# Moving the query weights to the head of the load stream, and the query ahead of the first key transposes

## Chip, cores and metric

The kernel runs on one core of one Trainium2 chip. The metric is device microseconds of one execution. Before the change the median is 190.97 us (5 runs, 190.83 to 191.34). Of the 95 executions on record, 91 lie within 0.3% of the median of their set; the widest set on record, 11 runs of before, spans 190.66 to 191.81. Every run of this study is on record as fast, so fast runs are compared with fast runs. The experiments ran on two chips, on which before has medians of 190.82 to 190.87 us.

## The reference

One decode step of a gated mix of attention and a small feed-forward network, for 8 rows `x` of 448 numbers:

```python
g = sigmoid((x * gate_w).sum(-1, keepdims=True))
# attention: 16 query heads, 8 key/value heads of 256, the last 1024 positions of the cache
q = (x @ wq)                      # wq is 448 x 4096, 3.67 MB
p = softmax(q . k * 256**-0.5)    # for each batch row and head
a = (p . v) @ wo                  # wo is 4096 x 448
# feed-forward: 448 -> 1792 -> 448
b = gelu(layernorm(x) @ w1 + b1) @ w2 + b2
out = g * a + (1 - g) * b         # 8 x 1 x 448, bf16
```

The window of keys and values is 8 x 8 x 1024 x 256 in bf16, 33.5 MB each. There is little arithmetic for so many bytes.

## The kernel before

All large loads go through one ring of nine slots of 16 KB per partition, issued by the sync engine (SP) in the order of a plan. A slot is loaded again when the entry nine places earlier has been used up (`done`).

```python
def pump():
    while len(slots) < min(len(plan), consumed[0] + RING):     # RING = 9
        t = ring.tile([P, SLOT], BF16, tag="slot", name="slot")
        plan[len(slots)](t)
        slots.append(t)
...
add_kv("k", A_k_cache, 0, parts=2)                     # first keys, 2 transfers of 1 MB
add(("wq", 0), rows_loader([wq_m[:, 0 : 2 * HD]]))     # query weights, 3 transfers, 3.67 MB
add(("wq", 1), rows_loader([wq_m[:, 2 * HD : 3 * HD], wq_t]))
add(("w1",), rows_loader([w1_m, w1_t]))
add(("w2",), rows_loader([w2_v]))
for u in range(1, NQ):                                 # NQ = 16 units of 4 key/value heads
    add_kv("k", A_k_cache, u)                          # 2.1 MB
    if u >= LAG:                                       # LAG = 2
        add_kv("v", A_v_cache, u - LAG)                # 2.1 MB
...                                                    # the last values, then wo in 6 pieces
```

Each unit's keys are turned by VectorE in two halves (`turn_keys`), multiplied by TensorE (`scores`), and used for softmax and values two units later. The query goes through TensorE, ScalarE and VectorE in turn:

```python
def turn_keys(u, hf):
    ...
    nc.vector.transpose(kt[...], kn[:, hf * CH * Dh : (hf + 1) * CH * Dh].bitcast(WORD))
    if hf == NH - 1:
        done()

def query():
    for r in range(NR + 1): ...   # 32 matmuls with wq, into Sq
    done(2)
    nc.scalar.activation(qs[:], Sq[:], ACT.Copy, scale=qscale)
    ...                           # 8 TensorE transposes, 4 VectorE copies (qd), 8 matmuls (qp)
    ...                           # 8 copies into the query tile qw, ScalarE and VectorE in turn

norm_and_gate()
for hf in range(NH):
    turn_keys(0, hf)
query()
hs = mlp_hidden()
for hf in range(NH):
    scores(0, hf)
mlp_out(hs)
for u in range(1, NQ): ...        # the steady state
...                               # the last units, then the output projection with wo
```

## Time and profile before

| | before |
|---|---|
| time, median | 190.97 us |
| span of the profiled run | 189.3 us |
| bytes read from HBM | 77.68 MB |
| load stream by the packet records, first to last byte | 182.8 us, 425 GB/s |
| TensorE / VectorE busy | 71% / 68% |
| last unit's keys landed, first transpose starts | 162.1 us |

The page of before, its slice rows and its chain (the work that ended last, followed back step by step to what released it). Each slice is 4.7 us; a digit is the busy share in tenths. PE is TensorE, PEld its weight loads, DVE VectorE, ACT ScalarE and POOL GpSimd.

```profile
span 189.3 us, 2502 instructions
PE 134.2 (71%) x1013; PEld 69.8 (37%) x1022; DVE 128.1 (68%) x186; ACT 43.1 (23%) x91; POOL 5.0 (3%) x7
...
DMA  5999999999999999999999999999999999999980
GB/s 188 422 424 434 428 435 431 422 422 440 429 433 429 426 436 426 429 436 433 429 426 433 428 436 422 433 433 426 436 426 433 436 426 426 436 433 426 410 356 14
...
DMA 84%; PE 8%; DVE 3%; ACT 1%; SPq 1%; issue 1%; ACTq 0%
```

No compute engine is above 71%, while the DMA row is full from the second slice to the last but two and the rate under it hardly moves. Over the whole stream the rate is 425 GB/s, and the slices but the first and the last three read 422 to 440. (Single slices can read too high: a packet counts in the slice in which it starts, and one of 16 KB is worth 3.5 GB/s.) That there is little left in the rate is my estimate from this evenness; no run was made to raise it.

The early part, from the timeline of before: start, duration, engine, line, what it does, and in brackets how long the engine had stood idle and for whom.

```profile
12.89 4.49 DVE L357 STREAM_TRANSPOSE kt<-slot 128x2048 int32<-128x2048 int32 x2
13.56 1.88 PE L371 MATMUL Sq<-slot,xT 128*8 128x512 bf16 x16 [0.79 <-DMA slot<-in_A_wq_dram]
16.00 1.02 PE L371 MATMUL Sq<-slot,xT 128*8 128x512 bf16 x8 [0.56 <-DMA slot<-in_A_wq_dram]
17.22 1.03 PE L371 MATMUL Sq<-slot,xT 128*8 128x512 bf16 x8 [0.19 <-DMA slot<-in_A_wq_dram]
...
26.55 0.70 DVE L414 CAST qw<-qp 32x512 bf16<-32x512 f32 x1 [0.64 <-ACT qw L412]
...
30.73 2.31 DVE L357 STREAM_TRANSPOSE kt<-slot 128x2048 int32<-128x2048 int32 x1 [1.25 <-DMA slot<-in_A_k_cache_dram]
...
45.27 2.31 DVE L357 STREAM_TRANSPOSE kt<-slot 128x2048 int32<-128x2048 int32 x1 [2.08 <-DMA slot<-in_A_k_cache_dram]
```

The query matmuls do wait for their weights three times: this is what the change aims at. But the same list shows VectorE waiting for keys at 30.73 and again at 45.27: compute has caught up with the stream and is paced by landings from there on.

### The profile page before, as it was taken

What the parts mean: (1) busy time and instruction counts of PE and PEld (TensorE: products, weight loads), DVE (VectorE), ACT (ScalarE), POOL (GpSimd) and SP (SyncE); (2) the same over time, 40 slices, a digit from 0 to 9 for tenths busy, and PEclk for the clock granted to TensorE, in tenths of its full rate; (3) what the DMA queues carried; (4) which work ended last, traced back from release to release, by engine and by line L of the source; (5) the groups of instructions that cost most, each with busy time, mean ns of one, the idle gap of its engine ahead of it and who ended that gap; (6) DMA issues with size and microseconds to landing.
All of it is one profiled execution on the core that took longest, in us unless ns stands there. A gap on an engine that the chain in (4) does not pass through costs nothing.

```text
span 189.3 us, 2502 instructions
## 1 busy us (share of the span) xinstructions
PE 134.2 (71%) x1013; PEld 69.8 (37%) x1022; DVE 128.1 (68%) x186; ACT 43.1 (23%) x91; POOL 5.0 (3%) x7
## 2 busy tenths in 40 slices
PE   0036899894878588866669985977499839399772
PEld 0021784441434143424225431533153414153461
DVE  7866266995949494949494949494958686772610
ACT  2031220313040404040401340314004404004510
POOL 8100000000000000000000000000000000000000
PEclk9999999999699966999955897999858999756955
DMA  5999999999999999999999999999999999999980
GB/s 188 422 424 434 428 435 431 422 422 440 429 433 429 426 436 426 429 436 433 429 426 433 428 436 422 433 433 426 436 426 433 436 426 426 436 433 426 410 356 14
DMA packets 6733, 77.84 MB, mean 411 GB/s; under 512 B 945, under 2 KB 1346, under 8 KB 1986
## 3 DMA queue, kind: packets, MB, share of 16 engines
q1 hardware_dynamic: 6512, 77.67, 96.5%
q8 instruction: 7, 0.11, 0.2%
q10 hardware_dynamic: 210, 0.02, 0.1%
q14 instruction: 4, 0.03, 0.0%
HBM read 77.68 MB, written 0.01 MB: 410 GB/s over the span
## 4 chain that ended last, share of the span: by engine, by line
DMA 84%; PE 8%; DVE 3%; ACT 1%; SPq 1%; issue 1%; ACTq 0%
DMA slot<-in_A_k_cache_dram 77%; DMA slot<-in_A_wq_dram 7%; PE S L429 3%; PE A_ps L672 2%; PE PO L501 2%; DVE kt L357 1%; PE fin L531 1%; ACT E L458 1%; SPq L118 1%; DVE mx L441 1%; ACT first L510 1%; DVE ET L471 0%; SPq L134 0%; PE mz L449 0%; DVE os__1552 L516 0%
## 5 line engine op out<-in xcount | busy, mean ns | idle before, releaser
L357 DVE STREAM_TRANSPOSE kt<-slot 128x2048 int32<-128x2048 int32 x32 | 73.7, 2306 | 33.7 <-DMA slot<-in_A_k_cache_dram 33.7
L429 PE MATMUL S<-kt,qw 128*128 128x512 bf16 x256 | 72.9, 433 | 30.5 <-DVE kt L357 26.7
L429 PEld LDWEIGHTS <-qw 128*128 128x128 bf16 x256 | 27.0, 106 | 69.4 <-issue 49.4
L458 ACT ACTIVATE E<-S,nmx 128x1024 bf16<-128x1024 f32 x16 | 22.2, 1387 | 2.6 <-DVE nmx L455 2.6
L534 ACT CAST oT<-fin 128x16 bf16<-128x16 f32 x16 | 3.6, 226 | 79.8 <-PE fin L531 79.8
L501 PE MATMUL PO<-slot,ET 128*16 128x512 bf16 x256 | 20.0, 441 | 0.1
L441 DVE TENSOR_REDUCE mx<-S 128x1 f32<-128x1024 f32 x16 | 19.0, 1187 | 0.3 <-PE S L429 0.3
L510 ACT ACTIVATE first<-PO,own 128x256 f32<-128x256 f32 x16 | 7.6, 473 | 29.2 <-PE PO L501 28.2
L471 DVE STREAM_TRANSPOSE ET<-E 128x512 int32<-128x512 int32 x16 | 11.2, 697 | 2.2 <-ACT E L458 2.2
L449 PE MATMUL mz<-m,same 128*128 128x4 f32 x32 | 6.8, 284 | 4.2 <-ACT oT L534 4.1
L423 PE MATMUL S<-place,foreign 128*128 128x512 bf16 x23 | 9.4, 409 | 0.1
L482 PEld LDWEIGHTS den<-rowsum,rowden 128*128 128x128 f32 x32 | 7.3, 234 | 3.9 <-issue 1.7
L449 PEld LDWEIGHTS mz<-m,same 128*128 128x128 f32 x32 | 5.7, 219 | 6.1 <-ACT oT L534 5.3
L501 PEld LDWEIGHTS <-ET 128*16 128x16 bf16 x256 | 5.3, 94 | 5.5 <-issue 2.3
L423 PEld LDWEIGHTS <-foreign 128*128 128x128 bf16 x32 | 3.2, 99 | 9.7 <-issue 7.9
L482 PE MATMUL den<-rowsum,rowden 128*128 128x1 f32 x32 | 5.2, 232 | 0.4 <-ACT E L458 0.4
L414 DVE CAST qw<-qp 32x512 bf16<-32x512 f32 x4 | 2.7, 687 | 3.4 <-ACT qw L412 3.4
L371 PE MATMUL Sq<-slot,xT 128*8 128x512 bf16 x32 | 3.9, 616 | 1.5 <-DMA slot<-in_A_wq_dram 1.5
L493 ACT ACTIVATE rsel<-sel,rb 128x8 f32<-128x8 f32 x16 | 4.7, 295 | 1.1 <-DVE rb L492 1.1
L455 DVE TENSOR_REDUCE nmx<-mz 128x1 f32<-128x4 f32 x16 | 2.3, 146 | 3.5 <-PE mz L449 3.5
L292 POOL MEMSET qw<- 128x5120 bf16 x1 | 4.4, 4364 | 0.0
L443 DVE TENSOR_SCALAR m<-block,mx 128x4 f32<-128x4 f32 x16 | 3.7, 229 | 0.6
(135 smaller groups left out, 84.9 us busy)
## 6 DMA issues: line engine op xcount, KB each, us to landing
slot<-in_A_v_cache_dram SPq DMA_DIRECT2D x16, 2048.0 KB, 36.5
slot<-in_A_k_cache_dram SPq DMA_DIRECT2D x15, 2048.0 KB, 38.8
slot<-in_A_wo_dram SPq DMA_DIRECT2D x3, 896.0 KB, 30.7
slot<-in_A_k_cache_dram SPq DMA_DIRECT2D x2, 1024.0 KB, 7.1
slot<-in_A_wq_dram SPq DMA_DIRECT2D x1, 2048.0 KB, 11.5
slot<-in_B_w_dram SPq DMA_DIRECT2D x1, 1568.0 KB
slot<-in_B_w_dram SPq DMA_DIRECT2D x1, 1344.0 KB
slot<-in_A_wq_dram SPq DMA_DIRECT2D x1, 1024.0 KB, 13.2
```

The lines of the kernel that those rows point to most:

```text
L292: nc.gpsimd.memset(qw[:], 0.0)
L357: nc.vector.transpose(kt[:].rearrange("p c k x r -> p (c k x r)").bitcast(WORD), kn[:, hf * CH * Dh : (hf + 1) * CH * Dh].bitcast(WORD),)
L423: nc.tensor.matmul(S[u][:, cols], lhsT=foreign[:], rhs=place[:], start=True, stop=False)
L429: nc.tensor.matmul(S[u][:, cols], lhsT=qw[:, j, u, m * RQ : m * RQ + P], rhs=kt[:, :, k, :, par], start=False, stop=(k == NK - 1 and par = ...
L441: nc.vector.reduce_max(mx[:], S[u][:], axis=AXIS.X)
L449: nc.tensor.matmul(mz[:], lhsT=same[:], rhs=m4[:], start=True, stop=True)
L458: nc.scalar.activation(E[:].rearrange("p c x i -> p c i x"), S.pop(u)[:].rearrange("p (c i x) -> p c i x", i=PAIR, x=BLK), ACT.Exp, bias=n ...
L471: nc.vector.transpose(ET[:].rearrange("p c r i -> p (c r i)").bitcast(WORD), E[:].rearrange("p c x i -> p (c x i)").bitcast(WORD),)
L482: nc.tensor.matmul(den[u][:], lhsT=rowden[:], rhs=rowsum[:], start=True, stop=True)
L493: nc.scalar.activation(rsel[u][:], sel2[:], ACT.Copy, scale=rb[:])
L501: nc.tensor.matmul(PO[32 * t : 32 * t + PAIR * RQ], lhsT=ET[:, c, 0:RQ, :], rhs=vn[:, PAIR * c * Dh : PAIR * (c + 1) * Dh], start=(c < QUA ...
L510: nc.scalar.activation(first[:], PO[:, 0, :], ACT.Copy, scale=own[:, 0:1])
```

## The change

The intent: the query is needed before any score can be computed, so its weights should come first, and it should be computed while the first keys are still on their way. The keys then come as one transfer.

```diff
-    add_kv("k", A_k_cache, 0, parts=2)
     add(("wq", 0), rows_loader([wq_m[:, 0 : 2 * HD]]))
     add(("wq", 1), rows_loader([wq_m[:, 2 * HD : 3 * HD], wq_t]))
+    add_kv("k", A_k_cache, 0)
     add(("w1",), rows_loader([w1_m, w1_t]))
...
     norm_and_gate()
+    query()
     for hf in range(NH):
         turn_keys(0, hf)
-    query()
     hs = mlp_hidden()
```

## The prediction

> **What bounds the kernel now.** The load stream. The slice row of DMA reads 9 of 10 in all slices but the first and last, at 422 to 440 GB/s; by the packet records bytes move from 2.2 to 184.9 us, 77.66 MB at 425 GB/s. [...] The chain that ended last is 84% DMA. PE is busy 71%, VectorE 68%. VectorE waits for key landings (33.7 us in total before the key transposes). The last key slot lands at 162.1 us; then compute and the last 8 MB of loads run side by side and end together: last byte 184.9, last output-projection matmul 185.9, span 189.3.
>
> **What the change does.** No byte and no arithmetic is added or removed. (1) The 3.67 MB of query weights land 2.1 MB earlier: 2.1/0.425 = 4.9 us, so their parts land at about 8.6, 11.1 and 12.3 us, not 13.6, 16.0 and 17.2. (2) The first keys land near 17 us, in one transfer: one issue fewer (0.64 us, not critical), and 128 packets of 16 KB (0.61 us) for 256 of 8 KB (0.33): at most 0.3 us of stream time. (3) In VectorE's order the query's copies precede the first key transposes.
>
> From the timeline of the first 35 us: the query matmuls can start after the gate matmul, at 12.7 us, and need 3.9; cast 1.0, transposes 1.0, copies 1.5, picks 1.0, the eight alternating copies into the query tile 5.3. So it is ready at about 25.5 us instead of 27.2. But the two key transposes (2.3 us each), which filled VectorE's wait for the weights (12.9 to 17.4), now follow, ending at 27.8 and 30.1. The first scores start near 28, not 27.2, and the hidden layer's VectorE work moves from 27.3 to about 30. The second key slot lands at 30.7 as before; its transpose starts perhaps 1.5 us later. So early compute loses 1 to 2 us.
>
> **How much is critical.** None. A pair of loads takes 9.7 us, VectorE's work per pair about 7.3 (14.5 of each 20), so a lag of 2 us is gone after one or two units. The first keys' slot comes free about 30 us, delaying the issue of a load from 21 to about 30; what is issued by then lasts until about 53 us, so the stream never runs dry. The end is set by the same bytes.
>
> **Prediction: 190.9 us, 190.1 to 191.8 with chance 0.8.** Faster by over 2%: 0.01; within 2%: 0.97; slower: 0.02.
>
> **What would show it.** DMA full in all slices; no wait of the query matmuls for weights over 1 us; first key transpose near 25.5 us; first scores within 1.5 us of 27.2; VectorE waiting for key landings again by 45 us; last key landing within 0.5 us of 162.1; the same closing 27 us.
>
> **What would make it wrong.** The granted clock. It was half at about 163 to 174 us and from 180.6 us. [...] If its phase shifts, the closing chain, with little slack against the stream, could lose up to 3 us, or gain at most 1 before the last landing bounds it. Also wrong if a gap opens in the stream near 30 to 55 us.

## The result, and the profile after

| | before | after |
|---|---|---|
| time, median of 5 | 190.97 us | 191.13 us (190.96 to 191.40) |
| ratio | | 1.0008, 95% interval 0.9994 to 1.0023 |
| span of the profiled run | 189.3 us | 189.4 us |
| load stream, first to last byte | 182.8 us | 183.1 us |
| first matmul of keys and query | 27.57 us | 26.57 us |
| second unit's first key transpose | 30.73 us | 30.87 us |
| last unit's first key transpose | 162.08 us | 161.94 us |
| output issued | 186.29 us | 186.00 us |

A ratio is the mean time of one kernel's fast runs over that of the other's of the same rounds, so it is not quite the ratio of the medians quoted.

The page of after, the lines that answer to those of before:

```profile
span 189.4 us, 2510 instructions
PE 130.9 (69%) x1022; PEld 66.9 (35%) x1022; DVE 128.0 (68%) x186; ACT 43.2 (23%) x91; POOL 5.0 (3%) x7
...
DMA  6999999999999999999999999999999999999980
GB/s 216 411 443 418 433 431 429 436 419 422 443 433 440 419 419 440 436 436 415 433 436 431 426 422 440 433 436 426 419 440 433 443 422 415 440 433 422 418 338 4
...
DMA 70%; DVE 17%; PE 6%; ACT 2%; issue 1%; SPq 0%; ACTq 0%
```

The stream is as full as it was. The chain's share of DMA is lower, 70 for 84%, and yet nothing was gained: the chain follows one of several paths that end nearly together, and in the first 45 us it now happens to run mostly through VectorE.

The early part of after, from its timeline:

```profile
12.69 3.26 PE L371 MATMUL Sq<-slot,xT 128*8 128x512 bf16 x32
...
23.48 0.70 DVE L414 CAST qw<-qp 32x512 bf16<-32x512 f32 x1 [0.64 <-ACT qw L412]
24.21 4.50 DVE L357 STREAM_TRANSPOSE kt<-slot 128x2048 int32<-128x2048 int32 x2
...
28.74 0.28 DVE L564 TENSOR_TENSOR z<-hT,b_sb 128x112 f32<-128x112 f32 x1
...
30.87 2.28 DVE L357 STREAM_TRANSPOSE kt<-slot 128x2048 int32<-128x2048 int32 x1
...
44.79 2.31 DVE L357 STREAM_TRANSPOSE kt<-slot 128x2048 int32<-128x2048 int32 x1 [1.50 <-DMA slot<-in_A_k_cache_dram]
```

The change did what it meant to: the 32 query matmuls run in one piece and the query's last copy is done 3 us earlier. Then the two key transposes, which before had filled VectorE's wait for the query weights (12.89 to 17.38), stand behind the query, and the second unit starts at 30.87 instead of 30.73. By 44.79 VectorE waits for a landing again, and with that the difference of the early part has gone.

### The profile page after: what moved, and what is told of

Read it like the earlier page. It is cut to its first block, busy times and chain, and to the rows that moved or that the text cites. A ratio compares the mean times of both kernels' runs of the same rounds, so it can differ in the third digit from the quotient of the medians.

```text
span 189.4 us, 2510 instructions
## 1 busy us (share of the span) xinstructions
PE 130.9 (69%) x1022; PEld 66.9 (35%) x1022; DVE 128.0 (68%) x186; ACT 43.2 (23%) x91; POOL 5.0 (3%) x7
## 4 chain that ended last, share of the span: by engine, by line
DMA 70%; DVE 17%; PE 6%; ACT 2%; issue 1%; SPq 0%; ACTq 0%
DMA slot<-in_A_k_cache_dram 41%; DMA slot<-in_A_v_cache_dram 20%; DMA slot<-in_A_wo_dram 10%; DVE kt L357 8%; PE S L429 3%; PE Sq L371 2%; DVE xz L245 1%; ACT qw L412 1%; DVE mx L441 1%; DVE qw L414 1%; ACT qs L381 1%; DVE Sq L198 0%; PE qp L399 0%; PE qt L386 0%; DVE ET L471 0%
## 5 line engine op out<-in xcount | busy, mean ns | idle before, releaser
L429 PE MATMUL S<-kt,qw 128*128 128x512 bf16 x256 | 70.5, 423 | 33.3 <-DVE kt L357 30.7
L501 PE MATMUL PO<-slot,ET 128*16 128x512 bf16 x256 | 18.3, 410 | 0.1
L423 PE MATMUL S<-place,foreign 128*128 128x512 bf16 x32 | 13.0, 407 | 0.1
L482 PEld LDWEIGHTS den<-rowsum,rowden 128*128 128x128 f32 x32 | 6.8, 216 | 3.6 <-issue 1.4
L449 PEld LDWEIGHTS mz<-m,same 128*128 128x128 f32 x32 | 5.2, 203 | 6.1 <-ACT oT L534 5.3
L672 PE MATMUL A_ps<-slot,oP 128*8 128x112 bf16 x128 | 3.9, 291 | 0.4 <-DMA slot<-in_A_wo_dram 0.4
L390 DVE COPY qd<-qt 128x64 bf16<-128x64 bf16 x4 | 0.6, 218 | 4.8 <-PE qt L386 4.8
```

Source lines behind the costliest of these rows:

```text
L423: nc.tensor.matmul(S[u][:, cols], lhsT=foreign[:], rhs=place[:], start=True, stop=False)
L429: nc.tensor.matmul(S[u][:, cols], lhsT=qw[:, j, u, m * RQ : m * RQ + P], rhs=kt[:, :, k, :, par], start=False, stop=(k == NK - 1 and par = ...
L449: nc.tensor.matmul(mz[:], lhsT=same[:], rhs=m4[:], start=True, stop=True)
L482: nc.tensor.matmul(den[u][:], lhsT=rowden[:], rhs=rowsum[:], start=True, stop=True)
L501: nc.tensor.matmul(PO[32 * t : 32 * t + PAIR * RQ], lhsT=ET[:, c, 0:RQ, :], rhs=vn[:, PAIR * c * Dh : PAIR * (c + 1) * Dh], start=(c < QUA ...
```

## The experiments

The theory: the stream of 77.7 MB sets the time; the early compute has more slack than the change can use or cost. Rivals: the two halves of the change are each worth something and cancel; the early chain is critical; compute, with the stream beside it, sets the end. Each run is compared with runs of before on the same chip; numbers of after are those of its profile above.

### The new load order alone

```diff
 # on after
-    query()
     for hf in range(NH):
         turn_keys(0, hf)
+    query()
 # the first keys' slot is given back with the weights': done(3) in query, none in turn_keys(0, 1)
```

> New load order, old compute order (key transposes of unit 0 ahead of the query in VectorE's order). Theory (stream bounds, early compute has slack): 191.1 us, within 0.3% of before; first scores start near 28 us, since VectorE now waits for the first keys (17 us) before it can do the query's copies; VectorE waits for key landings again by 45 us; last key landing at 162 +- 0.5 us. Rival (the two halves of the change are each worth something and cancel): this half, by itself, is over 0.5% off, with the opposite sign to the compute-only run.

Measured: 191.14 us, ratio 1.0009 (0.9990 to 1.0028). VectorE now starts with a wait of 3.99 us for the first keys, the first matmul of keys and query starts at 28.48 us and the second unit at 30.36; the last unit's first transpose starts at 162.01. One point missed: VectorE waits for key landings again at 54.58 us, not by 45.

### The new compute order alone

```diff
 # on before
-    for hf in range(NH):
-        turn_keys(0, hf)
     query()
+    for hf in range(NH):
+        turn_keys(0, hf)
 # the weights' slots are given back with the first keys': done(3) in turn_keys(0, 1), none in query
```

> Old load order, new compute order. Theory: 191.1 us, within 0.3% of before, although the early compute is the worst of the four combinations: query tile at 27.2 us as before, then the two key transposes of 4.6 us, so first scores near 29.5 us and the second unit's first transpose near 33.5 us; absorbed by 55 us. Rival (halves cancel): over 0.5% slower here.

Measured: 190.91 us, ratio 1.0000 (0.9982 to 1.0017). First keys matmul at 29.61 us, second unit at 33.90, last unit's first transpose at 162.11. This is the worst of the four early parts, 3.2 us behind before at the second unit, and it costs nothing. With the run before it, this rules out two halves of 0.5% that cancel.

### One transfer for the first keys, alone

```diff
 # on before
-    add_kv("k", A_k_cache, 0, parts=2)
+    add_kv("k", A_k_cache, 0)
```

> Before with the first keys in one transfer only. Theory: 190.7 to 191.1 us; at most 0.3 us less stream time (128 packets of 16 KB for 256 of 8 KB); VectorE's first transpose waits for the whole slot, 15.0 us perhaps instead of 12.9, with no effect on the end.

Measured: 191.32 us, ratio 1.0020 (1.0001 to 1.0039). The expected 0.3 us of gain is not there: the stream takes 183.0 us for 182.8. If anything the kernel became 0.4 us slower. VectorE's first transpose did not start later either (12.88 us); the keys had landed by then. Where the small loss lies is taken up below, in the run with two transfers.

### 2.1 MB more in the stream

```diff
 # on after
     add_kv("k", A_k_cache, 0)
+    add_kv("unused", A_v_cache, 0)      # given back with the first keys' slot, never read
```

> After with a load of 2.097 MB that nothing reads, put in the stream behind the first keys. Theory (the stream's bytes set the time): 2.097 MB at 425 to 430 GB/s = 4.9 us more, 196.0 us. Rival (the closing compute chain or another compute chain sets the end, and the stream only runs beside it): clearly less than 4.9 us.

Measured: 195.50 us, ratio 1.0240 (1.0219 to 1.0261) to before. By the packet records the stream is 188.1 us long, 5.0 more than after's, and the output is issued at 190.87 for 186.00 us, 4.87 later: as expected. The median itself is 0.5 us short of the expected 196.0, and the span grew by only 4.4 us, since the stretch from the issue of the output to the end was 2.8 us here and 3.35 in after. No engine has work to do with these bytes; what they cost is stream time.

### Useless work ahead of the first key transposes

```diff
 # on after; N is 8, 16 and 32 in three kernels
     query()
+    idle = consts.tile([P, 8], F32)
+    wide = same[:].rearrange("p (o r) -> p o r", o=1).to_broadcast([P, 8, P])
+    for _ in range(N):
+        nc.vector.reduce_max(idle[:], wide, axis=AXIS.X)
     for hf in range(NH):
```

> After with 8 useless VectorE reductions over 128x1024 (about 1.2 us each, 9.5 us) ahead of the first key transposes. Theory (early compute has slack, given back by VectorE's idle time of about 2.4 us per unit): 191.1 us, within 0.3% of after; the transposes of unit 0 start near 34 us, VectorE waits for key landings again by about 85 us. Rival (the early chain from the query to the scores is on the critical path): up to 9.5 us longer.

> The same with 16 reductions, 19 us. The first keys' slot is then free near 48 us; the loads issued by then keep the DMA engines busy until about 53 us. Theory: still 191.1 us, within 0.5%. Rival (early chain critical): up to 19 us longer.

> The same with 32 reductions, 38 us. The first keys' slot is free near 67 us, some 14 to 17 us after the last issued load has run out: a gap in the stream of that length and the same loss at the end: 205 to 209 us. If it is far less, the slack is larger than my estimate of 22 us; if it is the whole 38 us, there is no slack.

Measured: 193.12 us with 8 (ratio 1.0130), 193.07 with 16 (1.0127), 207.08 with 32 (1.0847). The first two miss the expectation by 2 us, and oddly by the same 2 us for a delay of 10 and of 20 us. The third is inside its range, but with the same 2 us in it. Its slice rows show the gap in the stream that was expected (slices of 5.1 us):

```profile
DMA  6999999999930199999999999999999999999980
GB/s 222 412 450 414 428 422 428 425 431 422 435 134 0 51 409 387 425 435 425 431 431 419 435 425 423 422 431 425 423 422 438 425 422 425 435 422 416 418 330 11
```

The DMA engines ran dry one after another, the last at 59.75 us, and the next packet starts at 71.17, because the load that reuses the first keys' slot was only issued at 69.83. With 8 and 16 there is no gap at all, and the stream still took 184.8 and 184.9 us for 183.1: it ran at 420 for 424 GB/s from end to end. A delay in the early part hardly explains a lower rate to the end. What the three kernels have besides the delay is one new tile of 32 bytes per partition. It lies among the constants, and the ring of slots lies behind them: in the built programs (not in the traces, which hold no addresses) the ring starts at byte 44,032 of a partition (43 x 1,024) in after and at 44,064 in these.

### The 32 bytes alone, and the delay without them

```diff
 # shift: on after, and nothing else
+    consts.tile([P, 8], F32, name="unused")
```

```diff
 # aligned delay: 16 reductions, into an old tile whose values nobody needs any more
+        nc.vector.reduce_max(zrow[:, 0:8], wide, axis=AXIS.X)
```

> After with one unused tile of 32 bytes per partition among the constants, which moves the ring of load slots from a start at 44,032 bytes (a multiple of 1,024) to 44,064; no other change. The two delay kernels of 8 and 16 reductions both had such a tile, and both were 2 us longer with a stream that never stopped but ran at 420 instead of 424 GB/s. Theory (the landing address of the slots sets the packet time): 192.9 to 193.2 us, mean 16 KB packet 0.619 us as in those. Rival (the VectorE delay cost the 2 us): 191.1 us, packets at 0.615 us.

> The delay of 16 reductions (20 us) again, with their result put in an old tile that nobody reads any more, so the ring stays at 44,032. Theory (slack of the early compute is over 20 us): 191.1 us, within 0.3% of after. Rival (the delay cost the 2 us): 193.1 us.

Measured: 192.90 us for the shift, ratio 1.0101 (1.0084 to 1.0117); 191.24 us for the aligned delay, ratio 1.0019 (1.0006 to 1.0031), against 1.0008 of after. So the 2 us came with the shift, and a delay of 20 us ahead of all key transposes costs nothing that stands out of the noise: the two ratios differ by 0.1% with overlapping intervals, and the output is issued at 185.98 us for 186.00. VectorE's timeline with the aligned delay:

```profile
25.30 20.03 DVE L610 TENSOR_REDUCE zrow<-same 128x8 f32<-128x1024 f32 x16
45.25 4.49 DVE L357 STREAM_TRANSPOSE kt<-slot 128x2048 int32<-128x2048 int32 x2
...
113.30 2.31 DVE L357 STREAM_TRANSPOSE kt<-slot 128x2048 int32<-128x2048 int32 x1 [0.71 <-DMA slot<-in_A_k_cache_dram]
123.06 2.31 DVE L357 STREAM_TRANSPOSE kt<-slot 128x2048 int32<-128x2048 int32 x1 [2.77 <-DMA slot<-in_A_k_cache_dram]
```

Unit 0's transposes start 21 us later than in after. VectorE then hardly pauses (19.9 of 20 us busy from 60 to 80 us) and has caught up with the landings at 113 us. And three of the six windows of 20 us from 40 to 160 us, which hold nothing but the steady state. Columns: window, its length, busy time of PE, PEld, DVE, ACT and POOL, granted clock, DMA share, GB/s. First after, then the shift:

```profile
60.00:80.00 20.00, 14.54 (x90) 7.38 (x89) 14.53 (x17) 4.49 (x10) 0.00 (x0) 0.92 1.01 430
100.00:120.00 20.00, 12.74 (x85) 6.18 (x84) 14.09 (x18) 4.67 (x11) 0.00 (x0) 1.00 1.01 431
140.00:160.00 20.00, 14.88 (x88) 7.14 (x87) 14.02 (x16) 5.12 (x12) 0.00 (x0) 0.91 1.01 431
```

```profile
60.00:80.00 20.00, 14.34 (x87) 6.74 (x86) 14.42 (x17) 4.48 (x10) 0.00 (x0) 0.93 1.01 427
100.00:120.00 20.00, 14.97 (x88) 7.25 (x89) 13.86 (x17) 4.71 (x11) 0.00 (x0) 0.88 1.00 424
140.00:160.00 20.00, 16.79 (x91) 8.08 (x89) 14.41 (x17) 4.45 (x10) 0.00 (x0) 0.77 1.00 424
```

The shift lowers the rate in each of the six windows, by 2 to 7 GB/s, with VectorE's busy time within 0.5 us of after's. TensorE's granted clock (the column of the windows before the DMA share, as a share of full speed) differs as well, 0.77 to 0.93 with the shift and 0.82 to 1.00 in after, but does not go with the rate: the aligned delay has 429 to 432 GB/s at clocks of 0.80 to 1.00.

The 32 bytes moved not only the slots but also, in the builds, the compute tiles that lie behind the ring, so a rival is that these slow the loads. The packet records speak against it. From 28 to 44 us in the first delay of 16 and in the aligned one, only VectorE works, and the tile that it reads has the same address in both builds; the median packet of 16 KB takes 614 ns with the shifted ring and 611 with the aligned one (means 615.7 and 611.0). So what slows the loads is where they land, not the compute beside them. One thing stays open: the first two loads land in shifted slots too and still take 611 ns once running; the longer packets set in with the third load, at about 14 us.

The shift is at the same time a good test of the theory: the stream's rate fell by 1% (424 to 420 GB/s), and the time rose by 1%.

### After with the first keys in two transfers

```diff
 # on after
-    add_kv("k", A_k_cache, 0)
+    add_kv("k", A_k_cache, 0, parts=2)
```

> After with the first keys in two transfers again. In the profiles of the three kernels with one transfer (after, loads only, one transfer) the last 3.3 us run from the issue of the output to the end of the span; in the three with the number of transfers of before (before, compute only, extra load) it is 2.85 to 3.0. Theory: this closing term follows the number of transfers; here 2.9 us and a time 0.2 to 0.4 us under after's, 190.7 to 190.95 us. Rival (it is chance, or it comes from the load order): 3.3 us here too.

Measured: 190.79 us, ratio 0.9997 (0.9984 to 1.0011). From the issue of the output (186.16 us) to the end of the span (189.0) it is 2.8 us, as expected. Over all profiles of kernels with the full stream, the stretch is 2.8 to 3.0 us in the four that issue as many loads as before, and 3.3 to 3.4 us in the eight that issue one fewer. So a program with one load fewer ends some 0.4 us later after its output is issued; in the two light kernels of the next section the same difference is 0.2 us (2.8 and 3.0). The time itself agrees (ratio 0.9997 for 1.0008), but the intervals overlap, and this is no more than 0.2%. Why one transfer fewer makes the end longer is not settled: the records that I read do not show what the last stretch waits for.

### A light stream

To see the order where the stream does not hide it, two kernels load no values; their value matmuls read the key slot (a wrong result; the comparison with the reference is too coarse to see the attention's values). The second keys are moved ahead of the feed-forward weights.

```diff
 # on before, and on after
-        if u >= LAG:
-            add_kv("v", A_v_cache, u - LAG)
...
-        vn = slot("v", u)
+        vn = slot("k", u)
...
+    add_kv("k", A_k_cache, 1)
     add(("w1",), rows_loader([w1_m, w1_t]))
 # slots are given back later, in values: the first six in values(1); in the kernel on after,
 # those of the query weights still in query
```

> A stream that no longer bounds the kernel: the values are not loaded, the value matmuls read the key slot instead (a wrong result on purpose), so 44.1 MB, about 104 us of loads; the second keys are loaded ahead of the feed-forward weights, so that they have landed (about 22 us) before VectorE comes to them. Load and compute order of before. VectorE bounds: 157 to 163 us, second unit's first key transpose near 29.5 us.

> The same light stream with the load and compute order of after. If the order has a price of its own where the early compute is exposed: the second unit's first key transpose starts near 30.9 us, 1.4 us later than in the light kernel with the order of before, and the whole is 1 to 2 us longer. Rival (getting the query early is a gain that only the stream hid): 1 to 3 us shorter than it.

Measured: 155.55 us with the order of before (ratio to before 0.8148), 155.49 with that of after (0.8149). Neither expectation holds: the first was for 157 to 163 us with the second unit at 29.5, and it started at 32.95; the second was for a cost of 1.4 us or a gain, and there is neither (32.99). The chains show why, first of the light kernel with the order of before, then with that of after (start, duration, what):

```profile
6.52 18.63 DMA slot<-in_B_w_dram
25.19 2.68 PE hT L538 x42
27.87 2.92 PE hT L548 x28
31.33 3.41 PE S L423 x8
```

```profile
8.54 16.65 DMA slot<-in_B_w_dram
25.23 2.68 PE hT L539 x42
27.92 2.92 PE hT L549 x28
31.37 3.41 PE S L424 x8
```

With the second keys ahead of them, the feed-forward weights land at 25.2 us in both, TensorE takes the hidden layer before the scores, and the first scores start at 31.3 us whatever the query did. So my rearrangement put another landing in the way, and the pair does not measure the price of the order by itself. Nor do the two give their slots back at the same points. What the pair does show is that without the values' bytes the kernel takes 155.5 us, now with VectorE busy 82% of the span and the chain 64% on it: in before, the stream held back some 35 us of work that could have run earlier.

## Why the prediction was right

The time, 190.9 us predicted and 191.13 measured, lies inside the range, and the class (within 2%) was right.

- "The load stream" bounds the kernel: confirmed. 2.1 MB more moved the issue of the output by 4.87 us (4.9 expected), a stream 1% slower by its landing address cost 1%, and a stream without the values let the kernel run in 155.5 us.
- "How much is critical. None": confirmed, with a wide margin. The three variants of the early part moved the second unit between 30.4 and 33.9 us and the time between ratios 1.0000 and 1.0009. A delay of 20 us was absorbed, one of 40 us was not: it cost 14 us over the two shorter ones of the same landing address (207.08 for 193.07), so the slack at this place is about 26 us, against 22 by my estimate from the loads already issued.
- "VectorE waiting for key landings again by 45 us" (44.79), "last key landing within 0.5 us of 162.1" (161.94) and "the same closing 27 us" (27.4): as predicted. Only the "8 MB of loads" beside that stretch are too few: by the numbers of before it is about 9.7 MB (162.1 to 184.98 us at 425 GB/s).
- "Early compute loses 1 to 2 us": the mechanism was right, the size was not. The two transposes did move behind the query, but the query was ready at 24.2 us, not 25.5, so they started at 24.21. I had taken TensorE's steps at the durations of before: 3.9 us for the query matmuls, 1.0 for the transposes and 1.0 for the picks (the matmuls into `qp`); they took 3.26, 0.62 and 0.65. The `qd` copies, put at 1.5 us, took 0.62. The sum was also added up wrongly: the steps as listed lead from 12.7 to 26.4 us, not 25.5. So the first scores came 1.0 us earlier than in before, not later, and the second unit lost 0.14 us, not 1.5.
- "At most 0.3 us of stream time" for 128 packets of 16 KB in place of 256 of 8 KB: nothing was saved. The alone run's stream was 183.0 for 182.8 us. The 0.33 us that I had used for an 8 KB packet is a mean that includes the first dozen of the program, which took 0.6 to 1.05 us each. The median is 0.309 us, and that of 16 KB packets 0.611: by these, 128 for 256 saves 0.9 us of packet time, which over 16 engines is under 0.1 us (an estimate).
- The clock: its phase did shift. In the windows from 165 to 170 and from 170 to 175 us the granted clock was 0.50 and 0.63 in before, 0.57 and 0.75 in after, and the last projection began 1.3 us earlier, which fits, though no run changes the clock alone. Only 0.3 us of this reached the issue of the output, since the last landing bounds it, as the prediction said.

The end of before, then of after, from the timelines:

```profile
182.56 0.92 PE L672 MATMUL A_ps<-slot,oP 128*8 128x112 bf16 x32
...
185.93 0.33 DVE L690 SCALAR_TENSOR_TENSOR res<-A_ps,gg_s,mixb 128x112 bf16<-128x112 f32 x1 [1.93 <-PE A_ps L672]
```

```profile
181.24 0.92 PE L672 MATMUL A_ps<-slot,oP 128*8 128x112 bf16 x32
...
184.12 0.95 PE L672 MATMUL A_ps<-slot,oP 128*8 128x112 bf16 x24 [0.20 <-DMA slot<-in_A_wo_dram]
185.22 0.36 PE L672 MATMUL A_ps<-slot,oP 128*8 128x112 bf16 x8 [0.16 <-DMA slot<-in_A_wo_dram]
185.63 0.33 DVE L690 SCALAR_TENSOR_TENSOR res<-A_ps,gg_s,mixb 128x112 bf16<-128x112 f32 x1 [2.94 <-PE A_ps L672]
```

In after TensorE is early and waits for the last two pieces of `wo`. In before it is late enough not to: the last byte lands at 184.98 us and its matmuls end at 185.9, so there the closing compute ends last, by under a microsecond. That the medians lie only 0.16 us apart, within the noise, is partly luck: by the profiles the output was issued 0.29 us earlier and the stretch behind it was 0.36 us longer; the prediction allowed for the first and did not have the second.

## What to carry to other kernels

In this kernel the DMA row is full in nearly every slice, and the order of the early loads and of the work beside them decided only who waits where. In such a case ask first how many microseconds of loads are already queued at the moment in question: here a delay of 20 us, shorter than that, cost nothing that stands out (ratio 1.0019 for 1.0008). A wait that is plainly visible (the query for its weights) was worth nothing, because another engine waits for a later landing before the difference can reach the end (VectorE, by 44.79 us in after). And when an experiment adds a tile, look at where it pushes the load buffers: 32 bytes moved this kernel more than its whole change did (ratio 1.0101, and 1.0008 for the change).

## What the runs leave open

- The landing address. All that changed for the loads was where they land: the ring starts at byte 44,064, not 44,032, with 16 KB per packet. 424 became 420 GB/s (183.1 and 184.9 us for 77.66 MB) and the kernel 2 us slower (ratio 1.0101). By what mechanism, no run shows; one offset was tried.
- The clock before its first record. In before the PEclk row reads 9 in its first ten slices (47 us), yet the weight loads of the first score matmuls follow each other every 0.43 us up to 30.13 us, and from 30.69 us on eight of them take 1.61 us together. The first clock record of that trace belongs to about 30 us; the row shows full speed ahead of it. The trace holds no granted clock for that stretch, and no run shows why the weight loads come further apart in it.
- The closing stretch. It is 2.8 to 3.0 us from the issue of four output transfers of 1.8 KB to the end, and 3.3 to 3.4 us with one load fewer; no run here takes the stretch apart.
